# Decode of the weights in four parts at successive matmul groups, and two score banks taken from the other pair

## The chip, the cores and the metric

The kernel runs on one core of a Trainium2 chip. Five engines with instruction streams of their own work on it: PE (TensorE, matmul), DVE (VectorE), ACT (ScalarE), POOL (GpSimd) and SP (SyncE, which here issues every DMA). Each engine works through its own stream in the order in which it was written and waits on semaphores for the others. The metric is the device time of one execution in microseconds (us), here and in all that follows.

## The reference, cut to what matters

Two blocks follow each other. The first is a chunked state space scan over 4 batches, 8 heads, 768 tokens, with 32 values and a state of 16 per head. The second is a feed-forward block with a hard swish between two matmuls, over 3072 tokens, from 256 to 2048 to 256.

```python
def _attn_ref(x, a, B, C):            # x (4, 8, 768, 32), B and C (4, 8, 768, 16)
    log_a = np.log(np.clip(a, 1e-06, 1.0))
    for c in range(nc):
        cum = np.cumsum(la, axis=-1)
        L = np.exp(cum[:, :, :, None] - cum[:, :, None, :]) * causal
        CB = np.einsum('bhin,bhjn->bhij', Cc, Bc)
        y_intra = np.einsum('bhij,bhjd->bhid', CB * L, xc)
        y_inter = np.einsum('bhin,bhnd->bhid', Cc, state) * np.exp(cum)[:, :, :, None]
        y[:, :, sl] = y_intra + y_inter
        state = decay_full * state + sum over j of (Bc xc decay_from_j)

def _moe_ref(x, w_in, w_out):
    h = x @ w_in
    g = h * np.clip(h + 3.0, 0.0, 6.0) / 6.0
    return (g @ w_out).astype(np.float32)
```

The two weight matrices arrive as 64-bit floats and have to become 32-bit floats on the chip; the other inputs are 32-bit floats. That conversion is the "decode" which the change touches.

## The kernel before, in words

**Tiling.** The sequence is cut into six chunks of 128 tokens. A chunk holds all four batches, so the feed-forward block works on 512 tokens at a time. For each chunk `k` the input matmuls run over 16 column blocks `f` of `w_in` (`mlp_in`, line 379). Each gives a bank `h`, from which ACT makes `r` (line 389) and DVE makes `gT` (line 390). The output matmuls (`mlp_out`, line 393) sum over the 16 row blocks of `w_out`, one batch at a time.

**The scan.** `steps(c)` (line 407) is a generator that gives the scan of chunk `c` in seven pieces. The first two prepare: `ends` makes the chunk's edge terms, `turn` transposes B and C for two batches, and `decay` makes the decay matrix `L` of a batch (a causal mask on POOL, then exponentials on ACT). The next four handle one batch each: `scores` computes C times B into four banks `cb` (line 316) and multiplies them into `L` on DVE (line 324), and `mix` multiplies `L` with x on PE (line 345). `keep` (line 357) copies the result of two batches to `yT` on ACT (line 366) and the new state on DVE (line 369). `yT` is the input of `mlp_in`. Chunk 0 has nothing to run beside and stands ahead of all matmuls of the feed-forward block; the pieces of chunk `k + 1` are put between the matmuls of chunk `k`.

**The decode.** The weights are read in eight blocks of 1 MB: 0 to 3 are the columns of `w_in` for four `f` each, 4 to 7 the rows of `w_out` for four `f` each. Three buffers `raw` hold loaded blocks, so block `i + 3` can be loaded when block `i` has been read (`load_w`, line 101). A block is decoded in eight operations of 128 x 1024: ACT copies the top 16 bits out (line 152), DVE makes the upper mantissa (line 153) and the exponent (line 156) and sign (line 158), ACT shifts and clips the exponent with two Relus (lines 160 and 161), DVE puts sign and exponent together (the OR, line 167), adds the lower mantissa (line 168) and multiplies both into the weight (the product, line 182). They are issued in three functions `decode_a`, `decode_b` and `decode_c`.

**Order.** Nothing is planned by a program; the engines follow the order of the code (line 67 turns the planner off). Block 0 is decoded ahead of chunk 0's scan. Blocks 1 to 4 have their three functions behind `f` = 0, 1, 2, then 4, 5, 6, then 8, 9, 10, then 12, 13, 14 of chunk 0 (lines 452 to 462). Blocks 5 to 7 are decoded whole behind the output matmuls of the block ahead of them (line 473).

**PSUM.** There are eight banks: four in the pool `ps`, which `h`, `cb` and the transposes `t_ps` take in turn, two in `ps_o` for the output matmuls `o`, and two in `ps_y` for the scan's results.

Of the kernel before, what the change touches and what calls it, by code (L numbers as in the profile page):

```python
# [8 lines left out]
FP32 = mybir.dt.float32  # L9
U32 = mybir.dt.uint32  # L10
U16 = mybir.dt.uint16
BF16 = mybir.dt.bfloat16
AF = mybir.ActivationFunctionType
ALU = mybir.AluOpType
# [5 lines left out]
def kernel(  # L20
# [23 lines left out]
    nc = tc.nc  # L44
    P = 128
# [5 lines left out]
    NF = DF // P  # L51
# [11 lines left out]
    ps = ctx.enter_context(tc.tile_pool(name="ps", bufs=4, space=PSUM))  # L63
    ps_o = ctx.enter_context(tc.tile_pool(name="ps_o", bufs=2, space=PSUM))
# [31 lines left out]
    NP = 4  # L96
    FP = NF // NP
    NRAW = 3
    raws = {}

    def load_w(i):
        raw = loads.tile([P, NK * FP * 2 * P], U32, name="raw", bufs=NRAW)
        if i < NP:
            cols = slice(2 * i * FP * P, 2 * (i + 1) * FP * P)
            src = moe_w_in[:, cols].rearrange("(k p) f -> p k f", p=P)
            dst = raw.rearrange("p (k f) -> p k f", k=NK)
        else:
            r0 = (i - NP) * FP * P
            src = moe_w_out[r0:r0 + FP * P, :].rearrange("(k p) m -> p k m", p=P)
            dst = raw.rearrange("p (k m) -> p k m", k=FP)  # L110
        nc.sync.dma_start(out=dst, in_=src)
        raws[i] = raw
# [13 lines left out]
    bias_hi = const.tile([P, 1], FP32, name="bias_hi")  # L126
    nc.vector.memset(bias_hi, 1151.0 * 2 ** 7)
    bias_lo = const.tile([P, 1], FP32, name="bias_lo")
# [4 lines left out]
        out=head, in_=head, pattern=[[-N * HU, 2], [-N, HU], [0, D]], compare_op=ALU.is_ge,  # L133
        fill=0.0, base=0, channel_multiplier=1)
    nc.gpsimd.affine_select(
        out=head, in_=head, pattern=[[N * HU, 2], [N, HU], [0, D]], compare_op=ALU.is_ge,
        fill=0.0, base=N - 1, channel_multiplier=-1)


    halves = {}  # L140

    def decode_a(i):

        n = NK * FP * P
        top = raws[i].bitcast(U16).rearrange("p (n w) -> p n w", w=4)[:, :, 3]
        hi = raws[i].rearrange("p (n w) -> p n w", w=2)[:, :, 1]
        s = att.tile([P, n], U16, name="ws")
        e = att.tile([P, n], U16, name="we")  # L150
        m = att.tile([P, n], U32, name="wm")
        nc.scalar.copy(out=s, in_=top)
        nc.vector.tensor_scalar(
            out=m, in0=hi, scalar1=0xFFFFF, scalar2=0x100000,
            op0=ALU.bitwise_and, op1=ALU.bitwise_or)
        nc.vector.tensor_scalar(  # L156
            out=e, in0=s, scalar1=0x7FF0, scalar2=None, op0=ALU.bitwise_and)
        nc.vector.tensor_scalar(
            out=s, in0=s, scalar1=0x8000, scalar2=None, op0=ALU.bitwise_and)
        nc.scalar.activation(e.bitcast(BF16), e, AF.Relu, bias=bias_hi, scale=-8.0)  # L160
        nc.scalar.activation(e, e.bitcast(BF16), AF.Relu, bias=bias_lo, scale=-1.0)
        halves[i] = s, e, m

    def decode_b(i):
        s, e, m = halves[i]
        lo = raws.pop(i).rearrange("p (n w) -> p n w", w=2)[:, :, 0]
        nc.vector.tensor_tensor(out=e, in0=e, in1=s, op=ALU.bitwise_or)
        nc.vector.scalar_tensor_tensor(  # L168
            out=m.bitcast(FP32), in0=lo, scalar=2.0 ** -32, in1=m, op0=ALU.mult, op1=ALU.add)
        if i + NRAW < 2 * NP:  # L170
            load_w(i + NRAW)

    def decode_c(i):
        s, e, m = halves.pop(i)
        m, e = m.bitcast(FP32), e.bitcast(BF16)
        if i < NP:
            dst = w_in[:, :, i * FP * P:(i + 1) * FP * P]
            m, e = (t.rearrange("p (k f) -> p k f", k=NK) for t in (m, e))
        else:
            dst = w_out[:, (i - NP) * FP:(i - NP + 1) * FP, :]  # L180
            m, e = (t.rearrange("p (k f) -> p k f", k=FP) for t in (m, e))
        nc.vector.scalar_tensor_tensor(  # L182
            out=dst, in0=m, scalar=2.0 ** -20, in1=e, op0=ALU.mult, op1=ALU.mult)
# [6 lines left out]
        out=a_sb, in0=a_sb, scalar1=1e-6, scalar2=1.0, op0=ALU.max, op1=ALU.min)  # L190
    nc.scalar.activation(a_sb, a_sb, AF.Ln)
    nc.vector.tensor_tensor_scan(
        out=flat, data0=run.rearrange("g c p -> g (c p)"), data1=a_sb, initial=0.0,
# [39 lines left out]
    for t in range(2):  # L233
        nc.gpsimd.tensor_tensor(
            out=parity[:, t:t + 1], in0=mask[:, t, 0:1], in1=mask[:, 2 + t, 0:1], op=ALU.add)
# [17 lines left out]
    def decay(c, b):  # L253

        L = Ls[c, b]
        if c > 1:
            by_j = cum_n[:, c, b * NH:(b + 1) * NH].unsqueeze(2).to_broadcast([P, NH, P])
            nc.gpsimd.tensor_tensor(out=L, in0=L, in1=by_j, op=ALU.add)  # L258
        nc.gpsimd.affine_select(  # L259
            out=L, in_=L, pattern=[[0, NH], [1, P]], compare_op=ALU.is_ge,  # L260
            fill=-1e5, base=0, channel_multiplier=-1)
        if c > 1:
            nc.scalar.activation(L, L, AF.Exp)  # L263
        else:
            decay_exp(c, b, L, 0, NH)
# [44 lines left out]
    def scores(c, b):  # L310
        bT, cT, csT = bTs[c, b // 2]
        cbs = []
        for q in range(NQ):
            rows = slice(32 * q, 32 * q + 32)
            cb = ps.tile([P, 2, P], FP32, name="cb", tag="f")
            nc.tensor.matmul(  # L316
                out=cb.rearrange("j h i -> j (h i)"), lhsT=bT[rows, b % 2],
                rhs=cT[rows, b % 2].rearrange("n t i -> n (t i)"), start=True, stop=True,
                tile_position=(32 * q, 0))
            cbs.append(cb)  # L320
        L = Ls[c, b]
        for q in range(NQ):
            hs = slice(2 * q, 2 * q + 2)
            nc.vector.tensor_tensor(out=L[:, hs], in0=L[:, hs], in1=cbs[q], op=ALU.mult)  # L324
# [68 lines left out]
    def mlp_out(k, b, f0, f1):  # L393
        if f0 == 0:
            outs[k, b] = ps_o.tile([P, DM], FP32, name="o", tag="o")
        o = outs[k, b]
        for f in range(f0, f1):
            nc.tensor.matmul(  # L398
                out=o, lhsT=gTs[k][:, f, b * P:(b + 1) * P], rhs=w_out[:, f],
                start=(f == 0), stop=(f == NF - 1))  # L400
        if f1 == NF:
            ob = ffn.tile([P, DM], FP32, name="ob", bufs=3)
            nc.scalar.copy(out=ob, in_=o)  # L403
            r0 = b * S + k * P
            nc.sync.dma_start(out=out[r0:r0 + P, :], in_=ob)

    def steps(c):

        ends(c)
        turn(c, 0)  # L410
        decay(c, 0)
        yield
        turn(c, 1)
        decay(c, 1)
        yield
        for b in range(NB):
            scores(c, b)
            if c + 1 < NC:
                load_decay(c + 1, b)
            if b + 2 < NB:  # L420
                decay(c, b + 2)
            if b:
                mix(c, b - 1)
            if b == 2:
                keep(c, 0)
            yield
        mix(c, 3)
        keep(c, 1)
        if 0 < c < NC - 1:
            load_eto(c + 1)  # L430

    def decode(i):
        decode_a(i)
        decode_b(i)
        decode_c(i)

    def load(c):
        load_bc(c)
        load_x(c)


    decode_a(0)
    by_token()
    decode_b(0)
    decode_c(0)
    load(1)
    load_eto(1)
    for _ in steps(0):
        pass


    weave = {}
    for i in range(1, 5):
        for j, part in enumerate((decode_a, decode_b, decode_c)):
            weave[0, 4 * (i - 1) + j] = part, i
    for k in range(NC):
        todo = steps(k + 1) if k + 1 < NC else iter(())
        for f in range(NF):
            mlp_in(k, f)
            if (k, f) in weave:  # L460
                part, i = weave[k, f]
                part(i)
            if f in (9, 13):
                next(todo, None)
        if k + 2 < NC:
            load(k + 2)
        next(todo, None)
        if k == 0:
            for i in range(NP):
                for b in range(2):  # L470
                    mlp_out(0, b, i * FP, (i + 1) * FP)
                if i + 1 < NP:
                    decode(NP + i + 1)
                    next(todo, None)
        else:
            for b in range(2):
                mlp_out(k, b, 0, NF)
                next(todo, None)
            mlp_out(k, 2, 0, NF // 4)
            next(todo, None)  # L480
            mlp_out(k, 2, NF // 4, NF)
        if k == 0:
            mlp_out(k, 2, 0, NF)
        next(todo, None)
        mlp_out(k, 3, 0, NF)

# [29 lines left out]
```

## Time and profile before

| what | us |
|---|---|
| median of 3 runs (lowest, highest) | 460.6 (460.03, 462.75) |
| the profiled execution, its own time | 462.3 |
| its span, first to last instruction | 460.6 |
| PE busy | 413.2 |
| DVE busy | 159.4 |
| ACT busy | 149.5 |
| POOL busy | 70.1 |

The span is read from the profiler's record of one execution. A line such as `L182` is the line of the kernel that issued an instruction. An entry like `[3.50 <-DVE w_in L182]` says that the engine stood idle for 3.50 us before this instruction and that DVE's write of `w_in` ended the wait. The clock in the profile is the share of full speed that was granted to PE; its mean over the span is 0.967.

### The profile page before, as it was taken

What the parts mean: (1) busy time and instruction counts of PE and PEld (TensorE: products, weight loads), DVE (VectorE), ACT (ScalarE), POOL (GpSimd) and SP (SyncE); (2) the same over time, 40 slices, a digit from 0 to 9 for tenths busy, and PEclk for the clock granted to TensorE, in tenths of its full rate; (3) what the DMA queues carried; (4) which work ended last, traced back from release to release, by engine and by line L of the source; (5) the groups of instructions that cost most, each with busy time, mean ns of one, the idle gap of its engine ahead of it and who ended that gap; (6) DMA issues with size and microseconds to landing.
All of it is one profiled execution on the core that took longest, in us unless ns stands there. A gap on an engine that the chain in (4) does not pass through costs nothing.

```text
span 460.6 us, 4992 instructions
## 1 busy us (share of the span) xinstructions
PE 413.2 (90%) x1948; PEld 260.1 (56%) x1948; DVE 159.4 (35%) x289; ACT 149.5 (32%) x268; POOL 70.1 (15%) x61
## 2 busy tenths in 40 slices
PE   2495684796999999999999999999999999999997
PEld 1242232364874467764467764477854487844786
DVE  5536545768014432213422113422124512034100
ACT  5544544863014521114521024520025510133200
POOL 2401014010000650000830000942500000000000
PEclk9998775999899999999999999999999999999999
DMA  8897422492027002236003255003100000000000
GB/s 154 255 293 192 158 83 91 102 166 99 23 60 123 0 1 70 105 60 111 1 0 94 90 69 92 0 26 118 49 14 2 0 13 12 13 11 0 1 23 23
DMA packets 87607, 32.23 MB, mean 70 GB/s; under 512 B 75584, under 2 KB 81408, under 8 KB 87584
## 3 DMA queue, kind: packets, MB, share of 16 engines
q1 hardware_dynamic: 87584, 31.92, 28.3%
q8 instruction: 15, 0.25, 0.2%
q14 instruction: 8, 0.07, 0.0%
HBM read 28.67 MB, written 3.24 MB: 69 GB/s over the span
## 4 chain that ended last, share of the span: by engine, by line
PE 58%; issue 18%; DVE 6%; SPq 6%; ACT 5%; POOL 3%; DMA 3%; POOLq 0%; ACTq 0%
PE o L398 32%; PE h L384 19%; SPq L210 3%; PE cb L316 2%; SPq L84 2%; DMA bc<-in_B_dram 2%; PE y L345 2%; DVE gT L390 2%; ACT r L389 1%; PE y L339 1%; ACT L L225 1%; POOL L L259 1%; DMA eto<-cum_d 1%; POOL L L258 1%; ACT we L160 1%
## 5 line engine op out<-in xcount | busy, mean ns | idle before, releaser
L384 PE MATMUL h<-yT,w_in 128*128 128x512 f32 x384 | 176.9, 618 | 16.3 <-DVE w_in L182 15.8
L398 PE MATMUL o<-w_out,gT 128*128 128x256 f32 x768 | 176.0, 388 | 4.6 <-DVE w_out L182 4.6
L398 PEld LDWEIGHTS o<-w_out,gT 128*128 128x128 f32 x768 | 146.2, 193 | 30.0 <-issue 5.3
L384 PEld LDWEIGHTS h<-yT,w_in 128*128 128x128 f32 x384 | 74.9, 198 | 107.6 <-issue 84.4
L390 DVE SCALAR_TENSOR_TENSOR gT<-r,h 128x512 f32<-128x512 f32 x96 | 65.2, 687 | 150.0 <-ACT r L389 150.0
L389 ACT ACTIVATE r<-h,half 128x512 f32<-128x512 f32 x96 | 64.3, 685 | 88.3 <-PE h L384 88.3
L403 ACT COPY ob<-o 128x256 f32<-128x256 f32 x24 | 9.0, 373 | 169.4 <-PE o L398 136.5
L324 DVE TENSOR_TENSOR L<-L,cb 128x256 f32<-128x256 f32 x96 | 34.1, 416 | 68.6 <-PE cb L316 68.5
L316 PE MATMUL cb<-cT,bT 32*128 32x256 f32 x192 | 25.6, 473 | 12.8 <-DVE cT L300 6.5
L282 POOL TENSOR_TENSOR tmp<-state,eto 128x512 f32<-128x512 f32 x4 | 4.2, 1048 | 191.9 <-ACT eto L279 191.9
L258 POOL TENSOR_TENSOR L<-L,cum_n 128x1024 f32<-128x1024 f32 x16 | 30.3, 1896 | 15.1 <-DMA L<-cum_d 15.1
L259 POOL TENSOR_SCALAR_AFFINE_SELECT L<-L 128x1024 f32<-128x1024 f32 x24 | 27.5, 1152 | 5.5 <-DMA L<-cum_d 4.2
L316 PEld LDWEIGHTS cb<-cT,bT 32*128 32x128 f32 x192 | 11.8, 203 | 26.2 <-DVE gT L390 10.5
L225 ACT ACTIVATE L<-L,cum_n 128x128 f32<-128x128 f32 x64 | 19.3, 389 | 7.1 <-POOL L L259 7.1
L263 ACT ACTIVATE L<-L 128x1024 f32<-128x1024 f32 x16 | 17.0, 1062 | 11.8 <-POOL L L259 11.8
L369 DVE TENSOR_TENSOR state<-y,mask 128x256 f32<-128x256 f32 x10 | 4.2, 424 | 37.0 <-ACT yT L366 37.0
L345 PE MATMUL y<-L,xt 128*32 128x128 f32 x384 | 16.7, 292 | 0.0
L366 ACT COPY yT<-y 128x256 f32<-128x256 f32 x24 | 7.8, 375 | 15.9 <-PE y L351 14.4
L273 POOL TENSOR_TENSOR bs<-bc,e_from 128x512 f32<-128x512 f32 x5 | 5.7, 1142 | 45.1 <-DMA bc<-in_B_dram 37.7
L160 ACT ACTIVATE we<-we,bias_hi 128x1024 bf16<-128x1024 uint16 x8 | 9.2, 1148 | 10.2 <-DVE we L156 10.2
L345 PEld LDWEIGHTS y<-L,xt 128*32 128x32 f32 x384 | 9.6, 114 | 4.8 <-issue 1.9
L168 DVE SCALAR_TENSOR_TENSOR wm<-raw,wm 128x1024 f32<-128x1024 uint32 x8 | 11.5, 1437 | 0.0
(46 smaller groups left out, 128.2 us busy)
## 6 DMA issues: line engine op xcount, KB each, us to landing
L<-cum_d SPq DMA_DIRECT2D x24, 512.0 KB, 5.5
raw<-in_moe_w_in_dram SPq DMA_DIRECT2D x4, 1024.0 KB, 8.3
raw<-in_moe_w_out_dram SPq DMA_DIRECT2D x4, 1024.0 KB, 5.2
xt<-in_x_dram SPq DMA_DIRECT2D x6, 512.0 KB, 6.7
out_dram<-ob SPq DMA_DIRECT2D x24, 128.0 KB, 1.7
bc<-in_C_dram SPq DMA_DIRECT2D x6, 256.0 KB, 5.5
bc<-in_B_dram SPq DMA_DIRECT2D x6, 256.0 KB, 7.5
eto<-cum_d SPq DMA_DIRECT2D x40, 32.0 KB, 1.9
```

What stands on the lines that cost most here:

```text
L210: nc.sync.dma_start(out=eto[h * N:(h + 1) * N], in_=cum_d[c, h:NB * NH:NH].unsqueeze(0).to_broadcast([N, NB, P]))
L225: nc.scalar.activation(Ls[c, b][:, h0 + q], src[:, q], AF.Exp, bias=cum_n[:, c, g:g + 1])
L258: nc.gpsimd.tensor_tensor(out=L, in0=L, in1=by_j, op=ALU.add)
L259: nc.gpsimd.affine_select(out=L, in_=L, pattern=[[0, NH], [1, P]], compare_op=ALU.is_ge, fill=-1e5, base=0, channel_multiplier=-1)
L263: nc.scalar.activation(L, L, AF.Exp)
L316: nc.tensor.matmul(out=cb.rearrange("j h i -> j (h i)"), lhsT=bT[rows, b % 2], rhs=cT[rows, b % 2].rearrange("n t i -> n (t i)"), start=Tr ...
L324: nc.vector.tensor_tensor(out=L[:, hs], in0=L[:, hs], in1=cbs[q], op=ALU.mult)
L345: nc.tensor.matmul(out=y_ps[u][32 * q:32 * q + 32, k], lhsT=xt[:, b * NH + h], rhs=L[:, h], start=(c == 0), stop=True, tile_position=(0, 3 ...
L384: nc.tensor.matmul(out=h, lhsT=w_in[:, j, f * P:(f + 1) * P], rhs=yTs[k][:, j].rearrange("p b i -> p (b i)"), start=(j == 0), stop=(j == N ...
L389: nc.scalar.activation(r, h, AF.Relu, bias=half, scale=1.0 / 6.0)
L390: nc.vector.scalar_tensor_tensor(out=gTs[k][:, f], in0=r, scalar=1.0, in1=h, op0=ALU.min, op1=ALU.mult)
L398: nc.tensor.matmul(out=o, lhsT=gTs[k][:, f, b * P:(b + 1) * P], rhs=w_out[:, f], start=(f == 0), stop=(f == NF - 1))
```

## The change

`decode` becomes one generator with the same eight operations, cut into four parts: the copy and the upper mantissa; exponent, two Relus and sign; lower mantissa, OR, and the load of block `i + 3`; the product. Within the second part the Relus are now written ahead of the sign, and in the third the lower mantissa ahead of the OR.

A helper `weights(i, n)` issues the next `n` parts of block `i`. The parts get new places:

- block 0 has two parts ahead of `by_token` and two behind it;
- block 1 has a part behind the scores of batch 2 and of batch 3 of chunk 0, one behind chunk 0's scan, and the last behind `f` = 0;
- blocks 2, 3 and 4 have one part behind each of `f` = 1 to 4, 5 to 8 and 9 to 12;
- block 5 has two parts behind the last `f` and two behind the first group of output matmuls; blocks 6 and 7 have their first two parts one group ahead of their last two.

In the scores of chunk 0, batches 1 and 3 take their first two banks from `ps_o` instead of `ps`.

```diff
-    def decode_a(i):
+    def decode(i):
...
         nc.vector.tensor_scalar(
             out=m, in0=hi, scalar1=0xFFFFF, scalar2=0x100000,
             op0=ALU.bitwise_and, op1=ALU.bitwise_or)
+        yield
         nc.vector.tensor_scalar(
             out=e, in0=s, scalar1=0x7FF0, scalar2=None, op0=ALU.bitwise_and)
+        nc.scalar.activation(e.bitcast(BF16), e, AF.Relu, bias=bias_hi, scale=-8.0)
+        nc.scalar.activation(e, e.bitcast(BF16), AF.Relu, bias=bias_lo, scale=-1.0)
         nc.vector.tensor_scalar(
             out=s, in0=s, scalar1=0x8000, scalar2=None, op0=ALU.bitwise_and)
-        nc.scalar.activation(e.bitcast(BF16), e, AF.Relu, bias=bias_hi, scale=-8.0)
-        nc.scalar.activation(e, e.bitcast(BF16), AF.Relu, bias=bias_lo, scale=-1.0)
-        halves[i] = s, e, m
-
-    def decode_b(i):
-        s, e, m = halves[i]
-        lo = raws.pop(i).rearrange("p (n w) -> p n w", w=2)[:, :, 0]
-        nc.vector.tensor_tensor(out=e, in0=e, in1=s, op=ALU.bitwise_or)
+        yield
         nc.vector.scalar_tensor_tensor(
             out=m.bitcast(FP32), in0=lo, scalar=2.0 ** -32, in1=m, op0=ALU.mult, op1=ALU.add)
+        nc.vector.tensor_tensor(out=e, in0=e, in1=s, op=ALU.bitwise_or)
         if i + NRAW < 2 * NP:
             load_w(i + NRAW)
-
-    def decode_c(i):
-        s, e, m = halves.pop(i)
+        yield
...
-            cb = ps.tile([P, 2, P], FP32, name="cb", tag="f")
+            if c == 0 and b % 2 and q < 2:
+                cb = ps_o.tile([P, 2, P], FP32, name="cb", tag="o")
+            else:
+                cb = ps.tile([P, 2, P], FP32, name="cb", tag="f")
...
+    parts = {i: decode(i) for i in range(2 * NP)}
+
+    def weights(i, n):
+        for _ in range(n):
+            next(parts[i], None)
+
+
+    weights(0, 2)
     by_token()
-    decode_b(0)
-    decode_c(0)
+    weights(0, 2)
     load(1)
     load_eto(1)
-    for _ in steps(0):
-        pass
-
-
-    weave = {}
-    for i in range(1, 5):
-        for j, part in enumerate((decode_a, decode_b, decode_c)):
-            weave[0, 4 * (i - 1) + j] = part, i
+    for i, _ in enumerate(steps(0)):
+        if i > 3:
+            weights(1, 1)
+    weights(1, 1)
+
+
+    weave = {0: 1}
+    for i in range(2, NP + 1):
+        for j in range(4):
+            weave[4 * i - 7 + j] = i
     for k in range(NC):
...
             mlp_in(k, f)
-            if (k, f) in weave:
-                part, i = weave[k, f]
-                part(i)
+            if k == 0 and f in weave:
+                weights(weave[f], 1)
...
+        if k == 0:
+            weights(NP + 1, 2)
         next(todo, None)
...
                 if i + 1 < NP:
-                    decode(NP + i + 1)
+                    weights(NP + i + 1, 2)
+                    if i + 2 < NP:
+                        weights(NP + i + 2, 2)
                     next(todo, None)
```

More of the change, by code (lines that the diff above doesn't have):

```diff
@@ L137 @@
         fill=0.0, base=N - 1, channel_multiplier=-1)
-    halves = {}
-    def decode_a(i):
+    def decode(i):
         n = NK * FP * P
         top = raws[i].bitcast(U16).rearrange("p (n w) -> p n w", w=4)[:, :, 3]
-        hi = raws[i].rearrange("p (n w) -> p n w", w=2)[:, :, 1]
+        lo, hi = (raws[i].rearrange("p (n w) -> p n w", w=2)[:, :, w] for w in range(2))
         s = att.tile([P, n], U16, name="ws")
@@ L430, in steps @@
             load_eto(c + 1)
[L432 to L435, printed above, removed]
     def load(c):
@@ L439, in load @@
         load_x(c)
-    decode_a(0)
+    parts = {i: decode(i) for i in range(2 * NP)}
[3 more added lines that the diff above has]
+    weights(0, 2)
     by_token()
-    decode_b(0)
-    decode_c(0)
+    weights(0, 2)
     load(1)
     load_eto(1)
-    for _ in steps(0):
-        pass
-    weave = {}
-    for i in range(1, 5):
-        for j, part in enumerate((decode_a, decode_b, decode_c)):
-            weave[0, 4 * (i - 1) + j] = part, i
+    for i, _ in enumerate(steps(0)):
[6 more added lines that the diff above has]
+            weave[4 * i - 7 + j] = i
     for k in range(NC):
@@ L472 @@
                 if i + 1 < NP:
-                    decode(NP + i + 1)
+                    weights(NP + i + 1, 2)
+                    if i + 2 < NP:
+                        weights(NP + i + 2, 2)
                     next(todo, None)
+            mlp_out(k, 2, 0, NF)
         else:
@@ L481 @@
             mlp_out(k, 2, NF // 4, NF)
-        if k == 0:
-            mlp_out(k, 2, 0, NF)
         next(todo, None)
```

## The prediction

> **What bounds the kernel now.** I read the page first, then the waits by total, then stretches of the span, then the time line.
>
> ```profile
> PE 413.2 (90%) x1948; PEld 260.1 (56%) x1948; DVE 159.4 (35%) x289; ACT 149.5 (32%) x268; POOL 70.1 (15%) x61
> ```
>
> ```profile
> PE h L384 <- DVE w_in L182: 15.8, 3, 7.1
> PE o L398 <- DVE w_out L182: 4.6, 2, 2.8
> ```
>
> PE is busy 90% of the span. The two waits (total, times, longest) are its waits for decoded weights. The stretches say where, and what else goes with it (length, busy PE, PEld, DVE, ACT, POOL, then the granted clock):
>
> ```profile
> 31.66:44.08 12.42, 7.13 (x17) 2.96 (x17) 7.54 (x11) 5.97 (x8) 1.15 (x1) 0.95 0.82 142
> 44.08:57.43 13.35, 9.85 (x17) 4.02 (x17) 6.81 (x11) 5.83 (x7) 0.00 (x0) 0.76 0.55 191
> 57.43:74.94 17.51, 10.45 (x21) 4.43 (x21) 9.90 (x13) 8.93 (x17) 6.68 (x5) 0.69 0.30 111
> 74.94:85.16 10.22, 10.22 (x21) 4.38 (x21) 3.68 (x7) 5.69 (x10) 0.00 (x0) 0.74 0.02 7
> 85.16:90.44 5.28, 2.45 (x10) 1.11 (x9) 5.28 (x10) 5.28 (x17) 0.00 (x0) 1.00 0.47 143
> 113.85:126.16 12.31, 12.31 (x50) 10.24 (x50) 1.27 (x4) 0.75 (x2) 0.00 (x0) 0.86 0.06 21
> 134.47:460.60 326.13, 317.79 (x1489) 202.86 (x1487) 89.44 (x172) 86.30 (x145) 52.61 (x37) 1.00 0.18 41
> ```
>
> The first four are chunk 0's input matmuls, four f each. The first needs 7.13 of PE, 1.78 per f; the four take 53.5 where 28.5 would do. From 134.47 on PE idles 8.3 in all, so what is won ahead of that moves the end one for one. Each wait also costs clock, shown by stretches laid on the places where the clock changed, 3.41 apart:
>
> ```profile
> 39.35:42.76 3.41, 0.00 (x0) 0.00 (x0) 2.89 (x4) 1.64 (x3) 0.00 (x0) 1.00 0.57 136
> 42.76:46.17 3.41, 2.09 (x3) 1.06 (x4) 1.86 (x3) 0.00 (x0) 0.00 (x0) 0.50 1.00 329
> 46.17:49.58 3.41, 3.41 (x5) 1.34 (x5) 0.96 (x2) 1.68 (x2) 0.00 (x0) 0.50 1.00 362
> 66.65:70.06 3.41, 1.22 (x3) 0.19 (x1) 3.41 (x3) 1.01 (x4) 2.93 (x3) 1.00 0.00 0
> 83.71:87.13 3.42, 2.08 (x6) 0.67 (x4) 3.06 (x5) 3.42 (x12) 0.00 (x0) 1.00 0.00 0
> 87.13:90.54 3.41, 1.92 (x7) 0.98 (x7) 3.41 (x7) 3.41 (x11) 0.00 (x0) 1.00 0.77 233
> 111.02:114.43 3.41, 0.60 (x5) 0.53 (x4) 3.38 (x6) 0.00 (x0) 0.00 (x0) 1.00 0.00 0
> ```
>
> A stretch in which PE was busy 0 to 1.92 of 3.41 is followed by half clock; one with 2.08 is not. Half clock lasts until one stretch is full. The first drop thus halves 44.08 to 49.58: 2.7 lost beside 5.3 idle.
>
> **The change, part by part.** I walk chunk 0 again with these durations (start, length):
>
> ```profile
> 47.90 0.69 ACT L389 ACTIVATE r<-h,half 128x512 f32<-128x512 f32 x1 [6.91 <-PE h L384]
> 48.48 1.10 ACT L152 COPY ws<-raw 128x1024 uint16<-128x1024 uint16 x1
> 48.62 0.69 DVE L390 SCALAR_TENSOR_TENSOR gT<-r,h 128x512 f32<-128x512 f32 x1 [4.00 <-ACT r L389]
> 49.22 0.69 DVE L153 TENSOR_SCALAR wm<-raw 128x1024 uint32<-128x1024 uint32 x1
> 49.83 0.42 DVE L156 TENSOR_SCALAR we<-ws 128x1024 uint16<-128x1024 uint16 x1
> 50.28 1.15 ACT L160 ACTIVATE we<-we,bias_hi 128x1024 bf16<-128x1024 uint16 x1 [0.69 <-DVE we L156]
> ...
> 52.52 1.25 ACT L389 ACTIVATE r<-h,half 128x512 f32<-128x512 f32 x2
> 53.82 0.69 DVE L167 TENSOR_TENSOR we<-we,ws 128x1024 uint16<-128x1024 uint16 x1
> 54.42 1.22 DVE L168 SCALAR_TENSOR_TENSOR wm<-raw,wm 128x1024 f32<-128x1024 uint32 x1
> 56.16 1.22 DVE L182 SCALAR_TENSOR_TENSOR w_in<-wm,we 128x1024 f32<-128x1024 f32 x1
> ```
>
> Start to start, gT, mask and OR take 0.6 each, mantissa and product 1.15, the exponent mask 0.45, the two Relus 2.24 until the next r. r starts 0.25 after its h (44.08 plus 2 x 1.78 at half clock, then 47.90).
>
> *Chunk 0's scores and decode 1.* (starts; the last four lines are the loads of the weights' blocks 1 and 4: issue, then time from issue to landing)
>
> ```profile
> 20.31 2.95 PE L316 MATMUL cb<-cT,bT 32*128 32x256 f32 x10 [3.77 <-DVE cT L300]
> 24.82 1.24 PE L316 MATMUL cb<-cT,bT 32*128 32x256 f32 x8
> 28.94 1.42 DVE L324 TENSOR_TENSOR L<-L,cb 128x256 f32<-128x256 f32 x4 [0.36 <-PE cb L316]
> 31.24 0.65 ACT L366 COPY yT<-y 128x256 f32<-128x256 f32 x2 [2.84 <-PE y L351]
> 31.66 0.70 PE L384 MATMUL h<-yT,w_in 128*128 128x512 f32 x1 [0.47 <-ACT yT L366]
> L111 SPq DMA_DIRECT2D raw<-in_moe_w_in_dram x1: 7187/7187/7187, 13.6 to 13.6; - x1
> DMA to landing us min/median/max: 12.1/12.1/12.1
> ...
> L111 SPq DMA_DIRECT2D raw<-in_moe_w_out_dram x1: 447/447/447, 42.4 to 42.4; - x1
> DMA to landing us min/median/max: 9.2/9.2/9.2
> ```
>
> Ten score matmuls took 2.95 at 20.31, where eight took 1.24 later: batch 1's banks were waited for. Ten without the wait are 1.55, so the other banks are worth 0 (if the products after them bind) to 1.4; I take 1.0, near the row. Batch 3's products, now also behind block 1's 0.69 mask on DVE, start at 28.2 and end at 29.6. The raw block landed at 25.7, before its copy on ACT would start (about 27.4), so that does not stall. But part 2 stands on ACT ahead of chunk 0's last yT copies: exponent mask until 30.0, two Relus until 32.25, yT then, input matmuls 0.42 later at 32.7, not 31.66. Cost 1.0; behind that wait stand the copies, and PE waits for them. If POOL slows the mask it is 1.8; if the Relus had gone first it would be -0.7; I take 1.0. PE then idles over 2 us, so a stretch near 1.9 busy is likely: one drop, 1.7 (half of 3.4; 0 to 2.7).
>
> *Input matmuls.* Decode 1 ends behind f=0 (products until about 37.2, PE needs them at 32.7 + 7.1): the 5.3 goes. Decode 2 is at f=1 to 4: r2 at 38.2, gT2, mask, Relus (0.72+0.6+0.45+2.24 = 4.0), r3 at 42.2. From there a group of four f is one chain over both engines: 0.72 + gT 0.6 + mantissa 1.15 + OR 0.6 + gT 0.6 + product 1.15 + gT 0.6 + mask 0.6 + gT 0.6 + 0.45 + 2.24 = 9.3, not 13.35: r7 at 51.5. The product is ready 4.9 after r3, at 47.1, when PE has just ended f=7 (32.7 + 8 x 1.78 = 46.9). Group three carries chunk 1's first step:
>
> ```profile
> 65.87 0.67 ACT L389 ACTIVATE r<-h,half 128x512 f32<-128x512 f32 x1
> 68.65 2.10 DVE L168 SCALAR_TENSOR_TENSOR wm<-raw,wm 128x1024 f32<-128x1024 uint32 x1
> 69.71 2.44 ACT L225 ACTIVATE L<-L,cum_n 128x128 f32<-128x128 f32 x8 [2.40 <-POOL L L259]
> 72.06 1.24 ACT L389 ACTIVATE r<-h,half 128x512 f32<-128x512 f32 x2
> ```
>
> r9 to r10 took 6.2 there, with the wait for POOL. So r9 at 52.7, copy 1.1, r10 at 60.0, then 4.0: r11 at 64.0. Then 0.72, gT 0.6, mantissa, OR, gT, product, gT (4.1), two transposed products (1.0, an estimate from gT's 0.69 for 512 columns), two gT: 71.8. PE's f=14 needs the bank that gT11 frees at 65.4 and idles about 3.5 before it: one drop, 1.7 beyond what the chain hides. gT ends at 73.5, scores about 1.0 later: the output matmuls begin at 74.5, not 90.44.
>
> *Output matmuls.* Mask and exponent of block 5 (1.05) put its Relus at 74.55 to 76.85. Then ACT alternates: exponentials 2.44, copy 1.1, exponent 0.45, Relus 2.3, exponentials 2.44, copy 1.1, 0.45, 2.3: 89.4. After that yT 0.65, state 0.8 (two operations of a size of which four took 1.42, rounded up), mantissa 1.2, OR 0.6, product 1.2: 93.8. The last block of output matmuls starts there instead of at 113.85: 20.0 earlier. Its 12.31 ran at 0.86 of the clock after a wait of 2.8; the wait left is about 1.8, so 1.2 (0 to 1.7) comes on top. On SP the loads keep their order: block 4's stands behind chunk 1's loads as before, so it lands at 51.6 again, and its copy comes behind r9, at 53.3. If it landed 5 later, ACT and with it the chain would wait 3.3.
>
> Sum: 20.0 + 1.2, less 1.7 for the drop at the start, less 0.9 for a DVE operation stretched by POOL (2.10 against 1.22): 18.6. The profiled execution took 462.3 (span 460.6 and 1.7 around it): 443.7. The median of the runs is 1.7 lower, 460.6: **442**. Its own range is 438 (no drops) to 447 (bank gain 0, one more drop of 2.7, one more stretch).
>
> The Trainium skill (TensorE: Matmul & The Clock Gate, "Why this matters for your kernels") asks only that PE has no idle gap over about 3 us, one idle window taking the clock down. The rows are stricter: 0.60 and even 1.92 busy of 3.41 fell, one after a gap of 2.8. By that rule the start keeps its clock.
>
> **The rivals.** *No drop at the start.* A gap of about 2.3 leaves a stretch over 2.08 busy if the grid's edge falls inside it. For: the edge is arbitrary. Against: 1.92 fell. Time 442 - 1.7 = 440. The skill's rule above would have this case.
>
> *Only the first wait goes.* r still stands behind the Relus, and if the chain per group stays 13 to 17, as now, only group one is won: 5.3 + 2.7 - 1.0, and the output part's 4.6 + 1.2: 12.8, 448. Against: 3.8 of the 13.35 is the restart at half clock (44.08 to 47.90), which is off the chain once the product is early.
>
> *The clock.* The waits become many of 1 to 2.5 instead of three long ones. If a drop falls at the start, in each of four input groups and each of four output groups, and PE runs two full stretches at half after each (3.4 lost), nine cost 30.6. The walk without its two drops ends at 442 - 2 x 1.7 = 438.6; with nine, 469, slower. It decides when over 1.4 of 3.41 idles about once in every group. Six or seven drops of 2.7 to 3.4 give 455 to 462, no change. Against: at half clock PE is the bound and fills its stretches.
>
> *The banks do nothing*: 1.0 more, 443, inside the range.
>
> **How the numbers follow.** Forecast 0.45, no drop at the start 0.2, first wait only 0.2, many drops 0.15, of which 0.09 within 1% and 0.06 slower. 1% is 4.6 us, about what a measurement of this kernel can tell from no change. Faster 0.85, same 0.09, slower 0.06. The range goes from 435 (438.6 without drops, less 0.9 without POOL's stretch, 1.7 with the Relus hidden at the start, 0.5 and 0.4 for the last block's clock and the banks at their best) to 452 (first wait only, with one more drop and one more stretch), and leaves out the many-drops case.
>
> **What would show it.** Right: the wait for w_in falls from 15.8 to under 2, that for w_out from 4.6 to about 2; first h near 32.7; r3 to r7 near 9.3; first output matmul near 74.5, last block near 94. Wrong: first h past 34, groups still 13 long with ACT waiting for PE, or three or more stretches at half clock between 30 and 95.

## The result, and the profile after

The changed kernel takes 442.3 us (median of four runs, 441.2 to 442.66) against 461.4 before (median with a fourth run; 460.6 was that of three): a ratio of 0.958, 95% interval 0.9545 to 0.9619. The profiled execution took 441.2, its span is 439.5. All times below are us.

From the page and from the waits of PE by total (total, times, longest):

```profile
PE 404.3 (92%) x1948; PEld 255.4 (58%) x1948; DVE 158.2 (36%) x289; ACT 149.4 (34%) x268; POOL 70.5 (16%) x61
```

```profile
PE h L381 <- DVE gT L387: 5.8, 4, 3.3
...
PE o L395 <- DVE w_out L176: 2.3, 2, 2.0
PE h L381 <- ACT yT L363: 2.2, 1, 2.2
...
PE h L381 <- DVE w_in L176: 0.4, 1, 0.4
```

The wait for `w_in` fell from 15.8 to 0.4, that for `w_out` from 4.6 to 2.3. Two waits are new or larger: 2.2 for the first `yT`, and 5.8 for banks that `gT` frees. The stretches, cut where PE resumes after a wait or starts a new group (length, busy PE, PEld, DVE, ACT, POOL, granted clock, DMA share, GB/s):

```profile
32.56:46.95 14.39, 14.01 (x33) 6.00 (x33) 11.24 (x16) 9.05 (x12) 1.06 (x1) 1.00 0.83 183
46.95:52.73 5.78, 4.13 (x12) 1.93 (x12) 3.24 (x7) 3.64 (x5) 0.00 (x0) 1.00 1.02 380
52.73:65.64 12.91, 8.50 (x20) 3.13 (x20) 8.76 (x13) 8.86 (x18) 6.67 (x5) 1.00 0.31 110
65.64:73.14 7.50, 6.91 (x16) 2.96 (x16) 6.91 (x11) 5.36 (x13) 0.00 (x0) 0.77 0.77 171
...
92.77:105.09 12.32, 12.32 (x50) 10.29 (x50) 1.27 (x4) 0.74 (x2) 0.00 (x0) 0.86 0.06 21
113.39:439.50 326.11, 317.79 (x1489) 202.85 (x1487) 89.37 (x172) 86.24 (x145) 52.56 (x37) 1.00 0.18 41
```

The first eight `f` run without a gap on PE. The input part ends with the first output matmul at 73.14, which was 90.44; the last block of output matmuls starts at 92.77, which was 113.85. From chunk 1's input matmuls on, the stretch is as long as before (326.11 against 326.13), so the 21.1 won by 92.77 is the 21.1 by which the span is shorter.

The chain that the prediction walked is seen best on ACT. `r` of f=3 starts at 42.03 and then, in the order of time:

```profile
42.03 1.82 ACT L386 ACTIVATE r<-h,half 128x512 f32<-128x512 f32 x3
```

```profile
51.29 1.82 ACT L386 ACTIVATE r<-h,half 128x512 f32<-128x512 f32 x3
53.00 1.14 ACT L151 COPY ws<-raw 128x1024 uint16<-128x1024 uint16 x1
54.02 0.65 ACT L273 ACTIVATE eto<-eto 128x512 f32<-128x512 f32 x1
54.55 0.38 ACT L292 COPY bT<-t_ps 128x256 f32<-128x256 f32 x1
57.86 2.44 ACT L219 ACTIVATE L<-L,cum_n 128x128 f32<-128x128 f32 x8 [2.93 <-POOL L L253]
60.21 0.67 ACT L386 ACTIVATE r<-h,half 128x512 f32<-128x512 f32 x1
61.97 1.15 ACT L158 ACTIVATE we<-we,bias_hi 128x1024 bf16<-128x1024 uint16 x1 [1.09 <-DVE we L156]
63.15 1.15 ACT L159 ACTIVATE we<-we,bias_lo 128x1024 uint16<-128x1024 bf16 x1
64.20 1.25 ACT L386 ACTIVATE r<-h,half 128x512 f32<-128x512 f32 x2
```

The lines with `r` are f=7 (51.29), f=10 (60.21) and f=11 (64.20). The group of four from f=3 to f=7 took 9.26. Between f=7 and f=10 stands the wait of 2.93 for POOL's mask, behind which `r` of f=10 is queued.

The clock, in stretches laid on the places where it changed (same columns):

```profile
28.09:31.51 3.42, 2.29 (x40) 1.11 (x32) 2.22 (x7) 1.98 (x3) 0.00 (x0) 1.00 1.27 282
...
62.22:65.63 3.41, 0.09 (x1) 0.00 (x0) 0.90 (x3) 3.38 (x5) 0.00 (x0) 1.00 0.00 0
65.63:69.04 3.41, 3.40 (x4) 1.51 (x5) 3.41 (x5) 2.99 (x10) 0.00 (x0) 0.50 0.23 36
89.54:92.95 3.41, 1.39 (x25) 0.83 (x24) 3.38 (x5) 0.00 (x0) 0.00 (x0) 1.00 0.02 5
92.95:96.36 3.41, 3.41 (x9) 2.70 (x10) 1.09 (x4) 0.00 (x0) 0.00 (x0) 0.50 0.00 0
```

It fell twice: after the gap ahead of f=14, and ahead of the last block, where a gap of 2.0 left 1.39 busy of 3.41. At the start of the input matmuls it did not fall in this execution: the edge between two stretches at 31.51 cut the gap in two, and 2.29 of the first stretch were busy.

### The profile page after: what moved, and what is told of

Its sections match the earlier page's. It is cut to its first block, busy times and chain, and to the rows that moved or that the text cites. A ratio compares the mean times of both kernels' runs of the same rounds, so it can differ in the third digit from the quotient of the medians.

```text
span 439.5 us, 4992 instructions
## 1 busy us (share of the span) xinstructions
PE 404.3 (92%) x1948; PEld 255.4 (58%) x1948; DVE 158.2 (36%) x289; ACT 149.4 (34%) x268; POOL 70.5 (16%) x61
## 4 chain that ended last, share of the span: by engine, by line
PE 61%; issue 15%; SPq 6%; ACT 5%; DVE 4%; POOL 4%; DMA 3%; POOLq 0%; ACTq 0%
PE o L395 34%; PE h L381 20%; SPq L204 3%; PE cb L313 2%; SPq L84 2%; DMA bc<-in_B_dram 2%; ACT L L219 2%; PE y L342 2%; DVE gT L387 2%; ACT r L386 2%; POOL L L253 1%; PE y L336 1%; DMA eto<-cum_d 1%; POOL L L252 1%; PE y L348 1%
## 5 line engine op out<-in xcount | busy, mean ns | idle before, releaser
L381 PE MATMUL h<-yT,w_in 128*128 128x512 f32 x384 | 170.7, 599 | 8.4 <-DVE gT L387 5.8
L381 PEld LDWEIGHTS h<-yT,w_in 128*128 128x128 f32 x384 | 72.4, 192 | 96.4 <-issue 80.2
L313 PE MATMUL cb<-cT,bT 32*128 32x256 f32 x192 | 23.8, 472 | 10.4 <-DVE cT L294 6.3
L313 PEld LDWEIGHTS cb<-cT,bT 32*128 32x128 f32 x192 | 10.8, 203 | 23.0 <-DVE gT L387 9.1
L219 ACT ACTIVATE L<-L,cum_n 128x128 f32<-128x128 f32 x64 | 19.3, 391 | 7.4 <-POOL L L253 7.4
L288 PEld LDWEIGHTS t_ps<-ident,bc 128*128 128x128 f32 x48 | 6.1, 153 | 8.9 <-DVE gT L387 5.2
```

The source lines that it names most:

```text
L219: nc.scalar.activation(Ls[c, b][:, h0 + q], src[:, q], AF.Exp, bias=cum_n[:, c, g:g + 1])
L313: nc.tensor.matmul(out=cb.rearrange("j h i -> j (h i)"), lhsT=bT[rows, b % 2], rhs=cT[rows, b % 2].rearrange("n t i -> n (t i)"), start=Tr ...
L381: nc.tensor.matmul(out=h, lhsT=w_in[:, j, f * P:(f + 1) * P], rhs=yTs[k][:, j].rearrange("p b i -> p (b i)"), start=(j == 0), stop=(j == N ...
```

## The experiments

The medians of one kernel differ by up to 0.7 from one comparison to the next (461.4 to 462.1 for the kernel before), and the runs of one kernel by 1 to 4, so effects under 1.5 are read from traces. A trace is one execution, and where its clock fell is part of it.

**The score banks.** All banks of chunk 0's scores from the old pool again:

```diff
-            if c == 0 and b % 2 and q < 2:
-                cb = ps_o.tile([P, 2, P], FP32, name="cb", tag="o")
-            else:
-                cb = ps.tile([P, 2, P], FP32, name="cb", tag="f")
+            cb = ps.tile([P, 2, P], FP32, name="cb", tag="f")
```

> The changed kernel, with all score banks of chunk 0 from the old pool again. Theory (the decode's chain over ACT and DVE sets the time, the banks bring the chain's start forward): everything from chunk 0's scores on is 1.0 us later, first input matmul at about 33.6 instead of 32.6, time 443.3 against 442.3. Rival (the banks do nothing, the products behind them bind): 442.3.

442.45 (ratio 0.959, 0.9562 to 0.9619). The theory had 443.3; the time doesn't tell this kernel from the changed one. The trace does: ten score matmuls, and the first input matmul. First without the new banks, then the changed kernel:

```profile
20.06 2.94 PE L310 MATMUL cb<-cT,bT 32*128 32x256 f32 x10 [3.73 <-DVE cT L294]
...
33.26 14.00 PE L378 MATMUL h<-yT,w_in 128*128 128x512 f32 x32 [2.17 <-ACT yT L360]
```

```profile
20.24 2.07 PE L313 MATMUL cb<-cT,bT 32*128 32x256 f32 x10 [3.64 <-DVE cT L294]
...
32.56 14.00 PE L381 MATMUL h<-yT,w_in 128*128 128x512 f32 x32 [2.18 <-ACT yT L363]
```

The ten take 2.94 instead of 2.07, and from them to the first input matmul it is 13.20 instead of 12.32. The banks are worth 0.9 there, and 0.7 at the end (spans of 440.2 and 439.5).

**Block 1 alone.** Blocks 2 to 4 at their old places, 5 to 7 whole, old banks:

```diff
-    weave = {0: 1}
-    for i in range(2, NP + 1):
-        for j in range(4):
-            weave[4 * i - 7 + j] = i
+    weave = {}
+    for i in range(2, NP + 1):
+        for j, n in enumerate((2, 1, 1)):
+            weave[4 * (i - 1) + j] = i, n
+    weave[0] = 1, 1
...
-                    weights(NP + i + 1, 2)
-                    if i + 2 < NP:
-                        weights(NP + i + 2, 2)
+                    weights(NP + i + 1, 4)
```

> Only block 1 of the weights is decoded early (in chunk 0's scan and behind f=0); blocks 2 to 4 start at f=4, 8 and 12 as before, blocks 5 to 7 stand whole behind the groups, and the banks are the old ones. Theory: the wait of 5.3 and its 2.7 of lost clock go, the Relus ahead of the last yT copies cost 2.0 (1.0 of it because the banks' gain is missing), so 6.0 off: about 455. The waits for w_in of blocks 2 and 3 stay, about 3.5 and 7. Rival (the first wait carries most of the gain): under 450.

452.5 (0.9804, 0.9773 to 0.9835): between the two theories. The waits of PE and the output part:

```profile
PE h L378 <- DVE w_in L176: 12.3, 2, 7.9
```

```profile
85.57 6.19 PE L392 MATMUL o<-w_out,gT 128*128 128x256 f32 x16
...
106.65 10.63 PE L392 MATMUL o<-w_out,gT 128*128 128x256 f32 x48 [1.55 <-DVE w_out L176]
```

The waits for blocks 2 and 3 stay, as the theory had it, and the first output matmul is 4.9 earlier (85.57 against 90.44). But the output part (from the first output matmul to the last block of them), whose places had not been touched, took 21.1 (85.57 to 106.65) instead of 23.4, and the last block 10.63 instead of 12.31. The 10.63 is the clock, which did not fall after this gap of 1.55. The 2.3 in the output part had no explanation yet.

**The output part as before, and the output part alone.** In the first the changed kernel decodes blocks 5 to 7 whole behind their groups (the last lines of the diff above, and the two parts of block 5 ahead of chunk 1's scores taken out). In the second the kernel keeps only the early halves of blocks 5 to 7.

> The changed kernel, with blocks 5 to 7 decoded whole behind their groups of output matmuls, as before. Theory: the first output matmul stays at 73.1, and from there to the last block it takes what it took before without its half clock, 21.7 instead of 19.6: 2.1 lost, 444.4. The wait for w_out is near 4.6 again. Rival (the output part is worth its whole wait and the clock lost with it, 5.8 as the prediction's second rival had it): 448.

> The kernel before, with only the early halves of blocks 5 to 7. Theory: the input part is as before, first output matmul near 90.4, and the output part takes 2 to 4 less: 457 to 459 against 461. Rival (5.8 as above): 455.

The first took 444.46 (0.9626, 0.9595 to 0.9658), the time that the theory gave. Its parts came out otherwise: in the trace the output part took 20.8 (76.00 to 96.82), not 21.7, the wait for `w_out` is 3.6, and the first output matmul came at 76.00, not 73.1, because the clock fell at the start and for two stretches ahead of f=14. So the early halves are worth 1.2 there (20.8 against 19.6), and the rest of the 2.2 between the medians isn't explained by them.

The second took 456.3 (0.9875, 0.9838 to 0.9912), less than the theory's 457 to 459; the 5.7 saved of 462 are the rival's 5.8. The trace does not bear the rival out: its execution is 4.1 shorter than the profiled one of before (spans of 456.5 and 460.6), 0.8 of it ahead of the first output matmul (89.65) and 3.3 in the output part, and the clock fell ahead of the last block all the same:

```profile
109.72 12.31 PE L392 MATMUL o<-w_out,gT 128*128 128x256 f32 x48 [1.50 <-DVE w_out L176]
```

Both share one thing with the experiment on block 1: the new order within the decode.

**The order within the decode.** The kernel before, with one exchange, and the changed kernel with it taken back:

```diff
-        nc.vector.tensor_tensor(out=e, in0=e, in1=s, op=ALU.bitwise_or)
         nc.vector.scalar_tensor_tensor(
             out=m.bitcast(FP32), in0=lo, scalar=2.0 ** -32, in1=m, op0=ALU.mult, op1=ALU.add)
+        nc.vector.tensor_tensor(out=e, in0=e, in1=s, op=ALU.bitwise_or)
```

> The kernel before, with only the lower mantissa issued ahead of the OR in the second function of the decode. In the two experiments that kept blocks 5 to 7 whole behind their groups (block 1 alone, output part as before) the stretch from the first output matmul to the last block took 21.1 and 20.8, not the 23.4 of before. Theory: the OR waits for the Relus, and the mantissa, behind it before, now runs while they do; each of the blocks 5 to 7 is ready about 1.1 sooner, the stretch takes about 20.8 and the time falls by 2 to 3, to about 459. Rival (the order is of no weight, the stretch got shorter because the clock stood better): no change, about 461.5.

> The changed kernel, with the OR ahead of the lower mantissa again. Theory: where the four parts are spread the Relus are done before the third part is issued or nearly so, so little is lost: block 6 ready 0.5 later, blocks 5 and 7 not late for PE; 442.3 to 442.8. Rival (the order carries 2 to 3 of the change's gain in the spread form too): 445.

The exchange alone takes the kernel before to 457.65 (0.9916, 0.989 to 0.9943): 4.5 off, where the theory had 2 to 3. Taken back in the changed kernel it doesn't show in the time, 441.7 (0.9574, 0.9545 to 0.9602). (The decode of a block is nine operations, not eight: three on ACT, six on DVE.) DVE in the decode of block 6, first before, then with the exchange:

```profile
102.16 0.69 DVE L167 TENSOR_TENSOR we<-we,ws 128x1024 uint16<-128x1024 uint16 x1 [1.94 <-ACT we L161]
102.77 1.22 DVE L168 SCALAR_TENSOR_TENSOR wm<-raw,wm 128x1024 f32<-128x1024 uint32 x1
104.03 1.23 DVE L182 SCALAR_TENSOR_TENSOR w_out<-wm,we 128x1024 f32<-128x1024 f32 x1
```

```profile
98.64 1.22 DVE L167 SCALAR_TENSOR_TENSOR wm<-raw,wm 128x1024 f32<-128x1024 uint32 x1
100.66 0.69 DVE L169 TENSOR_TENSOR we<-we,ws 128x1024 uint16<-128x1024 uint16 x1 [0.80 <-ACT we L161]
101.39 1.23 DVE L182 SCALAR_TENSOR_TENSOR w_out<-wm,we 128x1024 f32<-128x1024 f32 x1
```

Before, DVE waited 1.94 for the second Relu with the mantissa queued behind the OR; the product came 1.87 after the OR started. With the exchange the mantissa runs in that wait, and the product comes 0.73 after. Over three blocks that is 3.4; the output part took 3.5 less (90.13 to 110.08). The profiled execution is 5.5 shorter (spans of 455.1 and 460.6). Of that 0.3 stands ahead of the output part, and 1.7 is the last block, ahead of which the clock did not fall here:

```profile
110.08 10.63 PE L398 MATMUL o<-w_out,gT 128*128 128x256 f32 x48 [1.55 <-DVE w_out L182]
```

The seven traces side by side, with the output part, PE's wait for `w_out` ahead of the last block and the last block itself:

| kernel | output part | wait | last block |
|---|---|---|---|
| before | 23.4 | 2.81 | 12.31 |
| before, exchange alone | 20.0 | 1.55 | 10.63 |
| before, early halves and new order | 20.1 | 1.50 | 12.31 |
| block 1 alone, new order | 21.1 | 1.55 | 10.63 |
| changed | 19.6 | 2.02 | 12.31 |
| changed, output part as before | 20.8 | 1.68 | 12.31 |
| changed, exchange taken back | 20.6 | 1.75 | 10.63 |

In the output part of the kernel before, the exchange alone brings as much as the exchange and the early halves together, and in that of the changed kernel the exchange taken out costs 0.9 and the early halves 1.2. So they are in the main two ways to the same time, and their gains don't add; the early halves with the old order weren't run in the kernel before. In the changed kernel the exchange taken back makes DVE wait 0.61 for the second Relu in blocks 5 and 6, and PE waits 1.56 for block 6 instead of 0.29, more than the 0.5 of the theory. The 0.9 doesn't show in the time of that execution, as its last block took 10.63.

Whether the clock falls ahead of the last block doesn't follow from the length of the wait: it fell after 1.50 and 1.68 and stayed up after 1.55 and 1.75. The stretch with the wait in it was 1.92 busy after early halves and new order (it fell), and 1.85 with block 1 alone (it stayed up), in this order:

```profile
106.39:109.81 3.42, 1.92 (x33) 1.02 (x29) 3.38 (x5) 0.00 (x0) 0.00 (x0) 1.00 0.02 5
```

```profile
104.26:107.67 3.41, 1.85 (x25) 1.31 (x18) 2.99 (x6) 0.35 (x1) 0.00 (x0) 1.00 0.00 0
```

So near 1.9 of 3.41 the busy time of a stretch doesn't decide it either.

**The start.** Four matmuls of 256 columns that nobody reads, in the gap ahead of the first input matmul:

```diff
+    def fill(n):
+        for _ in range(2):
+            t = ps_o.tile([P, DM], FP32, name="fill", tag="o")
+            for _ in range(n):
+                nc.tensor.matmul(
+                    out=t, lhsT=w_in[:, 0, 0:P], rhs=w_in[:, 0, 0:DM], start=True, stop=True)
...
     weights(1, 1)
+    fill(2)
```

> The changed kernel with four matmuls of 256 columns that nobody reads, on PE between chunk 0's scan and the first input matmul, where it idled 2.2. Theory: the clock falls there in those runs in which the grid lies badly (mean clock 0.988 in three runs of the changed kernel, 0.992 in the profiled one, which was 1.0 to 1.5 faster); with the filler all runs are like the profiled one, clock 0.992, about 441.2. Rival (the lower clock in the other runs has another place): 442.3, clock 0.988 in most.

441.18 (0.9561, 0.9528 to 0.9594), with a clock of 0.992 in five of six runs, where the changed kernel had 0.988 in three of four and the experiment on the banks in three of six. That is as the theory has it, but 1.1 lies within the uncertainty, and the trace speaks for the rival. The profiled execution is the sixth run, with 0.987, and it did not lose its clock at the start: the first eight `f` took 14.00. Its clock fell ahead of f=14, as in the changed kernel, but for two stretches instead of one, so that f=14 and 15 took 6.22 instead of 5.37:

```profile
65.50 6.22 PE L381 MATMUL h<-yT,w_in 128*128 128x512 f32 x8 [3.34 <-DVE gT L387]
```

So a mean clock of 0.988 doesn't say where it was lost, and this experiment leaves that open. What a fall at the start costs is in other traces. The stretches at the start of the experiment with the output part as before, and then its first eight `f`:

```profile
28.91:32.33 3.42, 1.50 (x28) 0.86 (x24) 1.42 (x4) 2.36 (x3) 0.00 (x0) 0.99 1.16 184
32.33:35.74 3.41, 3.16 (x4) 1.51 (x5) 2.16 (x3) 0.47 (x2) 0.24 (x1) 0.51 0.93 92
```

```profile
32.58 15.52 PE L381 MATMUL h<-yT,w_in 128*128 128x512 f32 x32 [2.17 <-ACT yT L363]
```

With a stretch of 1.50 busy the clock fell, and the eight took 15.52 instead of 14.00; in the next experiment and in that with the exchange taken back it fell too, and they took 15.70. In the experiment on the banks it stayed up, with the same gap of 2.17.

**The gap ahead of f=14.** Six such matmuls behind chunk 1's second transposes:

```diff
             if f in (9, 13):
                 next(todo, None)
+            if k == 0 and f == 13:
+                fill(3)
```

> The changed kernel with six matmuls of 256 columns that nobody reads, on PE behind the second transposes of chunk 1 (after f=13), where it idled 3.3 and the clock then fell. Theory: no drop there, f=14 and f=15 run in 3.6 instead of 5.4; ACT's exponentials hide some of it, so last gT 1.1 to 1.7 earlier: 440.6 to 441.2. Rival (the chain hides all of the drop): 442.3.

441.27 (0.9558, 0.9523 to 0.9593), six runs from 439.05 to 442.13. The clock stayed up:

```profile
63.59 2.76 PE L437 MATMUL fill<-w_in 128*128 128x256 f32 x12
67.09 1.98 PE L381 MATMUL h<-yT,w_in 128*128 128x512 f32 x4 [0.75 <-DVE gT L387]
...
73.90 3.72 PE L395 MATMUL o<-w_out,gT 128*128 128x256 f32 x16
```

From f=14 to the first output matmul it is 6.81 here, 7.50 in the changed kernel. So this fall costs 0.7, less than the theory's 1.1 to 1.7; ACT's exponentials hide the rest. That is for one stretch at half clock, as in the changed kernel's profiled execution. Where it lasted two stretches, it took 8.34 (filler at the start) and 8.80 (output part as before), so up to 2.0.

**Block 1's Relus behind the yT copies, and the masks early.** Two attempts to shorten the chain, at its start and at the wait for POOL:

```diff
     for i, _ in enumerate(steps(0)):
-        if i > 3:
+        if i == 4:
             weights(1, 1)
-    weights(1, 1)
+    weights(1, 2)
```

```diff
+    for b in range(2):
+        causal(Ls[1, b])
+        masked.add((1, b))
     weave = {0: 1}
```

(`causal` is the `affine_select` of `decay`, which leaves it out for a batch in `masked`.)

> The changed kernel with block 1's second part (exponent, Relus, sign) behind chunk 0's last step instead of ahead of its yT copies. Theory: yT follows its matmuls at once, first input matmul at about 30.9 instead of 32.6; the Relus then hold r0 until 34.6, but r2, from which the chain starts, needs only its own h: 36.5 instead of 38.0. Time 440.7. Rival (the Relus only change places with the copies on ACT, and the chain starts where it did): 442.3.

> The changed kernel with POOL's causal masks of chunk 1's batches 0 and 1 issued ahead of the input matmuls instead of in chunk 1's first two steps. In the changed kernel ACT waits 2.9 for the first mask, and r10 stands behind that. Theory: r10 at 57.3 instead of 60.2, less up to 1.8 for DVE operations stretched by POOL at another place, and f=14 then waits little, so no drop: 439 to 441. Rival (what is won on ACT is lost again on DVE to POOL, or the next operand on the chain is late): 442.3.

The first took 440.8 (0.9548, 0.9516 to 0.958), the second 440.0 (0.9544, 0.9507 to 0.9581), both as their theories had it, and both within the uncertainty of the changed kernel's time. In the trace of the first the input matmuls start at 30.29 and `r` of f=3 at 40.85, 1.2 earlier; but `r` of f=10 comes at 59.76, only 0.45 earlier. The rest of the gain went to POOL:

```profile
53.76 1.22 DVE L176 SCALAR_TENSOR_TENSOR w_in<-wm,we 128x1024 f32<-128x1024 f32 x1
53.85 2.02 POOL L276 TENSOR_TENSOR tmp<-state,eto 128x512 f32<-128x512 f32 x1 [16.75 <-DMA raw<-in_moe_w_out_dram]
```

```profile
54.75 1.05 POOL L276 TENSOR_TENSOR tmp<-state,eto 128x512 f32<-128x512 f32 x1 [18.24 <-ACT eto L273]
54.93 1.95 DVE L176 SCALAR_TENSOR_TENSOR w_in<-wm,we 128x1024 f32<-128x1024 f32 x1
```

In the changed kernel (the second pair) this took 1.05, and DVE's product, which started 0.18 after it, took 1.95. Here the product started 0.09 before it and took 1.22, and POOL paid. The 0.45 was lost as well: the clock fell for two stretches ahead of f=14, the first output matmul came at 73.24, and the span is 439.5, that of the changed kernel. The 1.5 between the medians thus isn't shown by this trace. In the trace of the second ACT no longer waits for the mask, and `r` of f=10 starts 2.1 earlier:

```profile
55.74 2.48 ACT L219 ACTIVATE L<-L,cum_n 128x128 f32<-128x128 f32 x8
58.09 0.70 ACT L392 ACTIVATE r<-h,half 128x512 f32<-128x512 f32 x1
```

**Both, and both with filler.** The last one has `fill(2)` behind f=9 and f=13.

> The changed kernel with both late Relus of block 1 (as in the experiment on them) and early masks on POOL. Theory: the gains lie at different places of one chain and add, first input matmul at about 30.5, r10 near 56.9, time 442.3 - 1.5 - 2.3 = 438.5. Rival (the second step of the chain takes up what the first wins, by POOL and DVE standing in each other's way): 440.

> The same with four matmuls of 256 columns that nobody reads behind each of chunk 1's two transposes (f=9 and f=13), where PE idled 2.2 and 1.8. Theory: the clock stays up from f=10 on, one or two stretches at half clock less, of which the chain hid most before: 437 to 438.5 with a mean clock of 0.996. Rival (all hidden by the chain): as without them.

437.9 (0.949, 0.9462 to 0.9518) and 437.1 (0.9465, 0.9436 to 0.9495). By the medians the gains add (1.5 and 2.3 alone, 4.4 together), and both versions beat the changed kernel beyond the intervals (0.9518 and 0.9495 at most against 0.9545 at least). In the traces they add up to the first output matmul (69.95, with the masks alone 71.71, changed 73.14). The spans of both changes and of the masks alone are the same, 436.3 and 436.4, because the clock fell ahead of the last block in the one (12.31) and not in the other (10.63). The filler holds the clock at 0.996 in all four runs, but what it brings by itself, 0.8, is not resolved.

## Why the prediction was right, point by point

**The start.** Forecast 32.7 for the first input matmul, measured 32.56. The banks were taken at 1.0 and are worth 0.9. The copies of `yT` stood behind the Relus as the walk had it (wait of PE 2.2).

**The drop at the start.** It was put in at 1.7, with a rival for its absence. The profiled execution is the rival's case. Three traces with the same start fell there, at 1.5, 1.7 and 1.7, so the size was right; the changed kernel's own and three others with a gap of 2.2 kept the clock. The changed kernel's other three runs have the lower clock and are 1.0 to 1.5 longer, about one more stretch at half clock. No trace shows where they lost it: at the start, or ahead of f=14, where the two traces that kept the clock at the start and yet have 0.987 (the filler at the start, the late Relus) lost it for two stretches.

**The chain.** `r` of f=3, 7, 10 and 11: forecast 42.2, 51.5, 60.0, 64.0; measured 42.03, 51.29, 60.21, 64.20. This step carried most of the gain (17.3 of 21.1 are won by the first output matmul), and it held to 0.2 at each point. That it is the chain that binds is shown by the early masks, too: with POOL's wait gone from it, `r` of f=10 came 2.1 earlier.

**The gap ahead of f=14.** The clock fell there as forecast, at a cost of 0.7 beyond the chain instead of 1.7. That is the one term of the walk up to the output part that was mis-sized for this execution; other traces have up to 2.0. It and the scores' tail (0.7 instead of 1.0) put the first output matmul at 73.14 instead of 74.5.

**The output part.** From there to the last block 19.3 was forecast, and 19.6 came.

**The last block.** Here a step failed: 1.2 was to be won because the gap left was shorter, 1.8 instead of 2.8. It was 2.0, one stretch had only 1.39 busy, and the block took 12.31 again. The size is 1.7, but the length of the gap doesn't decide it in this range: after gaps of 1.55 and 1.75 the block took 10.63, after 1.50 and 1.68 it took 12.31. So a gap of 1.8 would not have made the term certain either. Nor is the rule that the prediction took from the rows of before, a fall after up to 1.92 busy, strict: with 1.85 busy the clock stayed up in one trace.

**POOL's stretch.** A DVE operation was stretched as supposed (the product at 54.93 took 1.95), but beside ACT's wait for the mask, on which `r` of f=10 hung, so the 0.9 cost nothing.

The sum for the profiled execution was 18.6: 20.0 up to the last block, + 1.2 - 1.7 - 0.9. Measured is 21.1 up to the last block and none of the other three. That is 443.7 forecast and 441.2 measured for the profiled execution, 2.5 off. The median was put 1.7 below the profiled execution and came out 1.1 above it, 2.8 the other way. So that the median came within 0.3 of 442 is luck; that the chain came within 0.2 is not.

**The rivals.** *Only the first wait* was priced at 12.8; done alone, block 1 brings 9.5, of which some 4 come from the order within the decode and from the last block's clock (2.3 and 1.7). It was refuted by groups of 9.26 in place of 13.35. *The clock* was refuted by two drops in place of nine; the lowest mean clock of the changed kernel, 0.988, is about three stretches at half clock, an estimate from 3.41 each in a span of 440.9. *No drop at the start*, which had a chance of 0.2, is what the profiled execution shows. *The banks do nothing* was refuted by 0.9 in the trace. The prediction gave the exchange of OR and mantissa no term of its own. For the changed kernel that cost about 0.9, as its trace without the exchange shows; that it is worth 4.5 by itself in the kernel before was not seen, and it is why the output part of the experiments with whole decodes came out shorter than the theory said.

## What to carry to other kernels

When several engines hand a value back and forth, find the period of that chain and add up its links from one operation of the kind to the next, as between two `r` here: DVE and ACT were about a third busy over the span, yet their chain set the time of this stage to within 0.2 at each point. Within a stream that is worked through in order, put what needs no late operand ahead of what waits, and try this first: one exchange of two lines gave the kernel before a quarter of what the whole rearrangement gave. Two changes that remove the same wait don't add, so measure each alone and also taken out of the whole.

## What the runs showed of the hardware that was not expected

The clock fell after stretches of 3.41 that were 1.39 and 1.50 busy, with gaps of PE of only 2.0 and 2.2, and it stayed up after one with 2.29 busy. The Trainium skill (TensorE: Matmul & The Clock Gate, "Why this matters for your kernels") names gaps over about 3 us; where it and these rows differ, the rows decide. With a gap of 2.2 at the start the clock fell in three traces (15.52, 15.70 and 15.70 for the first eight `f`) and did not in four (14.00 in each). Where the edge between two stretches lies in the gap sets how busy each stretch is: 1.50 and a fall in one trace, 2.29 and none in another. Near 1.9 this isn't decided by the busy time alone (1.92 fell, 1.85 did not), and what else counts stays open.

Where DVE's product and POOL's multiplication met, the one that started second was the one that became longer in the two traces shown: the product 1.95 instead of 1.22, or the multiplication 2.02 instead of 1.05. A shift of 0.3 in their order moved 0.7 to 1.0 from one engine's chain to the other's.
